# Twenty-four weight loads of an attention and feed-forward kernel: from SyncE's DMA queue to ScalarE's

## The chip, the core and the metric

The kernel runs on one core of a Trainium2 chip. The core has five engines that run side by side: TensorE (PE, matrix products, with its weight loads as PEld), VectorE (DVE), ScalarE (ACT), GpSimd (POOL) and SyncE (SP). SP computes nothing: it issues the transfers between main memory and the core's own memory, and 16 DMA engines carry them out. The metric is the device time of one execution in microseconds (us). Before the change the median of three runs is 685.02 us (681.62, 685.02 and 685.63).

## The reference, cut to what matters

Attention whose mask lets a query see only the keys that fall in the same hash bucket, then two gated feed-forward blocks:

```
q_bits, k_bits = (q @ proj > 0), (k @ proj > 0)          # 6 bits -> bucket
scores = where(q_bucket == k_bucket, q @ k.T / 8, -1e9)  # 2 x 8 heads, 768 x 768
attn   = softmax(scores);  x = attn @ v                  # head_dim 64
x = reshape(x, (1536, 512))
h = x @ w_in;  x = (h * sigmoid(h)) @ w_out              # 512 -> 2048 -> 512
a, b = x @ w1, x @ w2;  x = ((a * b) @ w3) @ w_out2      # 512 -> 1024 -> 1024 -> 512
```

## The kernel before, in words

The program is written as a list of some 2,900 small operations (`op(...)`), each with the engines that it may run on, what it depends on and which buffers it takes and gives back. No scheduler orders them at build time: a table of numbers, `ORDER`, gives the order in which they are written out, and a string, `ON`, gives each one's engine (P, A, D, G, S for PE, ACT, DVE, POOL, SP; N for none). `Plan.run` walks both. Every engine then works through its own operations strictly in that order; semaphores hold an operation back until what it needs is there.

The attention goes over eight pairs of heads, 12 tiles of 128 queries a pair. For each tile PE makes the scores (L763) into one of two `score` buffers, DVE takes the row maximum `st` (L779), ACT takes the exponential `P` (L785, with a short ACTIVATION_READ_ACCUMULATOR that ends it) and so frees the score buffer, and DVE turns `P` over into `pt` (L826). At the end of a pair PE multiplies `pt` with the values `V` (L884), and ACT moves the sums into `X` (L349, L902). Between these stand fillers for PE: the product of two weight matrices, `w3` and `w_out2` (L969), the first parts of the feed-forward (L1252, L1296), and plain transposes (L543).

The weights come in through `piece(...)`. Each half piece is a load of 512 KB (128 rows of 4 KB) into one of two buffers, `raw` (L385). ACT or POOL then reads it (`low`, L403 or L407), ACT reads it again (`high`, L398), and with that the buffer is free for the next load. DVE joins both into `x` (L413), and POOL (now and then ACT) rounds `x` into the two halves of `piece` (L353, L356), from which PE works. So a load into `raw` always waits for the L398 (and, where POOL made `low`, the L407) of the load that held the buffer before.

Before the change SP issues every transfer of the program, in one row: the loads of weights (L385), the queries, keys and values (`qraw`, `kraw`, `V`), the mask rows (`kb<-bits`, `qb<-bits`, L548), copies within the core (L713), the small stores and reads of the inverse sums (`inverse`, `invb`), the product of the weights (`wprime`), and the output. ACT issues none. A transfer that waits on SP holds up the ones behind it.

Of the kernel before, what the change touches and what calls it, by code (L numbers as in the profile page):

```python
# [194 lines left out]
    "ADADDASSSSPPPPPPDDDDAAANAGGGGANAADDPPNPPPPPPPDDDDDNSSSSGGAAAAGGGGGDSGNSSSNPPPPPDDDAAASSAANPPPPPPPNPP"  # L195
    "PPPDDDADDAAAANPPPPDDDDAAAGGGGSSSSSSSPPPPGGGGGDDDDAANAAANPPPNDDGDDDPPPAAANDDDASSNSSSGGGGAADDPPDAPPDDD"
    "GGGAGGAAPDAPDDDPPPAANAASSSNSSPDPPPNPPPDGGGGAAASSSDDDAANPPPPPDDDAAPDAPPPPPGGDDDADDSSSSSSSSSGGGNGGAANA"
    "DPPPDDDAANDDPNAADPDDAASSSSSNSGGAASGGGGPPPPPPDDAPAADDDDGGNPPPPDAANAPPPPPNDDDAASNSSSSSADDDASGGAGGGGGGG"
    "GGPPPPPPPPPPDADDDPDAAAAPPPPDDDDANADDDASSSSSSSSNAANPPPDPNDPPDDNSSSSSSNAAGGGGGGAADPPPPPPPDDDDAGAADAPDP"
    "DDAAAPPPPNPPPPPPPGDDDGGSSDNAAAAAANASSSSGGSSSSGGGGSSSSGPPDDDDAADDPPPPPADDDGGGANAANASPPPGDADANAPPPPNDD"  # L200
    "DDDDPPAANADAPPASSGGGGDDDGPPPPPPSNAAGSSDDDADDPAAADAGGNSSNGGSSSSSSSPPPDDPNDPPPPPPPAANAADDAADDGGGGAANSS"
    "SDPADDPPADAAPPPPPPDDDDSGGGSGGAAAAAANPPPPPNPPPDDDDDDAANDGDSSSSSNSSNAAGDDDPDPDAAAGGGGPDDPDGAAGGAPPPPPP"
    "DDDGAPNPPPDSSSAASSNSSSDDDDPAADPPAAPPPDDDAAGDANADDDADGGGGGPPPPPPPPDDDSSSSSSSGGAANADDSNNSPPNNAGGNGANAD"
    "DDDDAAAPPPPPPADDGGDDPPADPPPPADADDDAAAPPPPPPPSSSSSNSSADDADDAPPPDAGNGGGSSSPPNPAPPPDDDADDPPNPADDAAAPPPP"
# [60 lines left out]
class Plan:  # L265
# [10 lines left out]
    def op(self, on, emit, deps=(), due=0.0, take=(), give=(), size=0, port=False, kind=None, tiled=False):  # L276


        self.ops.append(Op(on, emit, deps, take, give))
        return self.ops[-1]  # L280
# [20 lines left out]
def lsh_attention_moe_kernel(ctx, tc, qT, kT, pair0, v, vt, w3, wo2, win, wo1, w12, out):  # L301
    nc = tc.nc
    ctx.enter_context(tc.manual_schedule())
    engine = {"PE": nc.tensor, "ACT": nc.scalar, "DVE": nc.vector, "POOL": nc.gpsimd, "SP": nc.sync}
    plan = Plan()
    op = plan.op
# [58 lines left out]
    def piece(src, need, wide=True, after=(), duo=False, late=None):  # L365
# [4 lines left out]
        for n in range(0, PIECE, STEP):  # L370
            due = need - 12.0 + 5.0 * n / STEP
            key = name + (n,)
            raw, x, t = key + ("raw",), key + ("x",), key + ("t",)
            first = [("piece", name)] if n == 0 else []
            c = slice(n, n + STEP)
            if wide:
                words = src.bitcast(U32)[:, 2 * n:2 * n + 2 * STEP]
# [7 lines left out]
                load = op({"SP": 400}, lambda e, raw=raw, words=words: nc.sync.dma_start(out=plan[raw], in_=words),  # L385
# [36 lines left out]
            else:  # L422
                load = op({"SP": 400}, lambda e, raw=raw, n=n: nc.sync.dma_start(
                    out=plan[raw].bitcast(F32)[:, :STEP], in_=src(n)), after, due - 10, [("raw", raw)], size=262144, kind="reload")
# [127 lines left out]
    for n in range(B * NPAIR):  # L552
# [4 lines left out]
        raw, hi, lo, ins = {}, {}, {}, []  # L557
# [395 lines left out]
    behind = [w for w, k in WINDOWS for _ in range(k)]  # L953
    after = lambda w: BEGIN + (12 * w + 19) * UNIT
    wo2p = [piece(wo2[i], after(behind[0]) - 8 + i) for i in range(4)]
    combined, before_it = [], None
    span = 5.5
# [248 lines left out]
    for cell in cells:  # L1206
# [75 lines left out]
        for order, (bk, d) in enumerate(turns_):  # L1282
# [29 lines left out]
                else:  # L1312
# [5 lines left out]
                    if halved:  # L1318
                        ev = None
                        for x in range(2):  # L1320
# [6 lines left out]
                            n = bk * 4 + d  # L1327
# [8 lines left out]
                if part == 2 and c == NOUT - 1 and not halved:  # L1336
                    n = bk * 4 + d
# [82 lines left out]
```

## Time and profile before

| | |
|---|---|
| median of three runs | 685.02 us (681.62 to 685.63) |
| the profiled execution, whole | 687.5 us |
| its span, first to last instruction | 685.7 us |
| mean granted TensorE clock | 0.995 |
| busy: PE, DVE, ACT, POOL | 669.0, 516.2, 376.7, 254.0 us |
| DMA moved | 65.3 MB, 95 GB/s on average |

The profile is of one execution. "Busy" leaves out the time in which a sequencer issues a transfer or waits. In a row of a timeline the numbers are start and duration, and what stands in square brackets at the end is the idle time of that engine just ahead, and what ended it. "Issue" there is idle time that ended with no semaphore that the profile shows. The profiled execution lies 2.5 us above the median of the unprofiled runs.

### The profile page before, as it was taken

How to read it: one execution, taken by the hardware profiler on the slowest of the kernel's cores; microseconds unless marked ns; L12 is line 12 of the kernel's file. 1: busy time of each engine (PE TensorE's matmuls, PEld its weight loads, DVE VectorE, ACT ScalarE, POOL GpSimd, SP SyncE). 2: the span in 40 equal slices, each digit the busy share in tenths (PEclk: the TensorE clock that was granted, in tenths of full speed). 3: DMA queues.
4: the chain of work that ended last, by engine and by line, in shares of the span. 5: the costliest groups of instructions: out<-in, count | busy, mean ns of one | idle time of the engine just before them, and what ended most of it. 6: DMA issues, size and time to landing. Idle time of an engine off the chain costs nothing.

```text
span 685.7 us, 13737 instructions
## 1 busy us (share of the span) xinstructions
PE 669.0 (98%) x5542; PEld 544.1 (79%) x5542; DVE 516.2 (75%) x739; ACT 376.7 (55%) x705; POOL 254.0 (37%) x263
## 2 busy tenths in 40 slices
PE   8899998999999999999999999999999999999997
PEld 6558787887787887888888888888887788888886
DVE  6889987796899887967686976778868575545475
ACT  5888776677767564577543553544545454322220
POOL 3668875777578331652200220211222244000000
PEclk9999999999999999999999999999999999999999
DMA  7576645445454611314320221110310012000004
GB/s 228 149 232 179 192 137 155 134 131 184 130 175 108 178 52 54 118 37 147 114 108 1 65 90 47 62 47 1 123 47 31 16 62 77 1 0 16 0 16 168
DMA packets 22031, 65.34 MB, mean 95 GB/s; under 512 B 3408, under 2 KB 4944, under 8 KB 21520
## 3 DMA queue, kind: packets, MB, share of 16 engines
q1 hardware_dynamic: 21968, 64.48, 30.8%
q8 instruction: 43, 0.70, 0.4%
q14 instruction: 20, 0.16, 0.1%
HBM read 55.19 MB, written 5.29 MB: 88 GB/s over the span
## 4 chain that ended last, share of the span: by engine, by line
PE 90%; DVE 5%; ACT 3%; issue 2%; POOL 0%; ACTq 0%; POOLq 0%; DVEq 0%
PE more L1296 21%; PE more L1132 15%; PE more L1252 9%; PE score L763 8%; PE acc L884 7%; PE acc L1296 7%; PE acc L969 6%; PE acc L1132 6%; PE acc L1252 4%; PE turn L884 2%; ACT P L785 1%; DVE st L779 1%; PE acc L850 1%; DVE pt L826 1%; PE acc L543 1%
## 5 line engine op out<-in xcount | busy, mean ns | idle before, releaser
L1132 PE MATMUL more<-y,piece 128*128 128x512 f32 x456 | 115.9, 390 | 0.6 <-DVE y L356 0.3
L785 ACT ACTIVATE P<-score,st 128x768 f32<-128x768 f32 x92 | 82.6, 899 | 41.4 <-DVE st L779 39.5
L779 DVE TENSOR_REDUCE st<-score 128x1 f32<-128x770 f32 x92 | 85.4, 943 | 20.8 <-PE score L763 19.3
L1132 PEld LDWEIGHTS more<-y,piece 128*128 128x128 f32 x456 | 85.4, 188 | 19.3 <-DVE sg L1149 0.9
L1296 PE MATMUL more<-gh,piece 128*128 128x512 f32 x268 | 94.1, 390 | 0.0
L1315 DVE SCALAR_TENSOR_TENSOR X<-more,X 128x512 f32<-128x512 f32 x88 | 59.9, 688 | 40.2 <-PE more L1296 39.6
L826 DVE STREAM_TRANSPOSE pt<-P 128x768 f32<-128x768 f32 x84 | 80.4, 965 | 6.6 <-ACT P L785 6.5
L884 PE MATMUL acc<-pt,V 32*64 32x193 f32 x1344 | 63.6, 328 | 4.9 <-issue 4.5
L884 PE MATMUL turn<-pt,V 32*64 32x193 f32 x1344 | 63.0, 329 | 0.2
L1252 PE MATMUL more<-x,piece 128*128 128x512 f32 x240 | 61.9, 390 | 0.0
L884 PEld LDWEIGHTS acc<-pt,V 32*64 32x64 f32 x1344 | 51.8, 132 | 12.2 <-issue 10.7
L1296 PEld LDWEIGHTS more<-gh,piece 128*128 128x128 f32 x268 | 50.3, 188 | 11.0 <-DVE sg L1198 0.3
L353 POOL TENSOR_SCALAR piece<-x 128x512 fp32r<-128x512 f32 x37 | 23.5, 639 | 83.3 <-DVE x L413 37.1
L1252 PEld LDWEIGHTS more<-x,piece 128*128 128x128 f32 x240 | 45.0, 188 | 9.6 <-DVE X L1315 0.3
L1296 PE MATMUL more<-gl,piece 128*128 128x512 f32 x134 | 52.1, 389 | 0.0
L969 PE MATMUL acc<-piece,piece 128*128 128x512 f32 x192 | 50.6, 401 | 0.0
L763 PE MATMUL score<-ka,qa 128*128 128x384 f32 x168 | 48.2, 369 | 2.4 <-ACT P L785 1.8
L413 DVE SCALAR_TENSOR_TENSOR x<-x,x 128x512 uint32<-128x512 uint32 x59 | 44.3, 754 | 6.2 <-ACT x L398 5.2
L349 ACT ACTIVATE sg<-more 128x512 f32<-128x512 f32 x28 | 16.6, 595 | 57.0 <-PE more L1132 38.0
L884 PEld LDWEIGHTS turn<-pt,V 32*64 32x64 f32 x1344 | 46.7, 132 | 1.4 <-issue 1.3
L1296 PE MATMUL more<-piece,gh 128*128 128x512 f32 x152 | 46.8, 389 | 0.0
L1132 PE MATMUL acc<-y,piece 128*128 128x512 f32 x174 | 45.8, 390 | 0.0
(234 smaller groups left out, 1426.2 us busy)
## 6 DMA issues: line engine op xcount, KB each, us to landing
raw<-in_w SPq DMA_DIRECT2D x27, 512.0 KB
raw<-in_wo SPq DMA_DIRECT2D x22, 512.0 KB
raw<-in_win SPq DMA_DIRECT2D x13, 512.0 KB
V<-in_v SPq DMA_DIRECT2D x14, 384.0 KB
invb<-inverse SPq DMA_DIRECT2D x16, 192.0 KB
out<-X SPq DMA_DIRECT2D x11, 256.0 KB
kraw<-in_kT SPq DMA_DIRECT2D x7, 384.0 KB
qraw<-in_qT SPq DMA_DIRECT2D x7, 384.0 KB
```

The source lines that it names most:

```text
L353: engine[e].tensor_scalar(out=dst, in0=src, scalar1=by, scalar2=1.0, op0=ALU.mult, op1=ALU.mult)
L413: engine[e].scalar_tensor_tensor(out=u32(x), in0=u32(x), scalar=3, in1=u32(t), op0=ALU.logical_shift_left, op1=ALU.bitwise_or)
L763: nc.tensor.matmul(out=sc[:, g, :HF], lhsT=lhs[:k, qs], rhs=rhs[:k, g * HF:g * HF + HF], start=(k == 128), stop=(k != 128),)
L779: nc.vector.tensor_reduce(out=plan[uk("st")][:, 0:1], in_=area()[:, :, :HF + 1], op=ALU.max, axis=AX.XY, negate=True)
L785: nc.scalar.activation(out=plan[uk("P")], in_=area()[:, :, :HF], func=AF.Exp, bias=s[:, 0:1], accum_out=plan[key("sums")][:, par * NQ + i: ...
L826: nc.vector.transpose(plan[mine][:, :, 32 * i:32 * i + 32], plan[uk("P")].rearrange("p g (b i) -> p (g b) i", i=32))
L884: nc.tensor.matmul(out=to[a][64 * side:64 * side + 64, :GW + 1], lhsT=V[rows_, c, side], rhs=plan[key(f"pt{side}")][rows_, c, :GW + 1], st ...
L969: nc.tensor.matmul(out=plan[key + ("ps",)], lhsT=w[:, a, k], rhs=r[:, c], start=(k == 0 and n == 0), stop=(k == 7 and n == 2),)
L1132: nc.tensor.matmul(out=plan[bk[b]], lhsT=w[:, a], rhs=y, start=(opens and j == 0 and m == 0), stop=(j == 1 and m == 2), skip_group_check=True)
L1252: nc.tensor.matmul(out=plan[key], lhsT=w[:, a], rhs=x, start=(k == 0 and n == 0), stop=(k == 3 and n == 2))
L1296: nc.tensor.matmul(out=plan[key], lhsT=a, rhs=x, start=(f == 0 and n == 0), stop=(f == 1 and n == 2))
L1315: nc.vector.scalar_tensor_tensor(out=dst, in0=plan[key], scalar=by, in1=dst, op0=ALU.mult, op1=ALU.add)
```

## The change

Twenty-four of the loads at L385 get the letter A in place of S, so ScalarE's sequencer issues them, on ScalarE's DMA queue. The load operation may now run on either engine:

```diff
-                load = op({"SP": 400}, lambda e, raw=raw, words=words: nc.sync.dma_start(out=plan[raw], in_=words),
+                load = op({"SP": 400, "ACT": 400}, lambda e, raw=raw, words=words: engine[e].dma_start(out=plan[raw], in_=words),
```

(the same for the reload at L423, of which none moves). In `ORDER` the 24 numbers stand earlier; one line of it:

```diff
-    917, 178, 116, 889, 896, 908, 909, 910, 115, 187, 918, 911, 897, 180, 184, 898, 899, 20, 900, 189, 16, 901, 231,
+    917, 178, 116, 889, 896, 908, 909, 910, 931, 115, 938, 187, 918, 911, 897, 180, 184, 898, 899, 20, 900, 189, 16,
```

The moved loads are those that SP issued between 51 and 237 us of the profiled execution: 12 of `w3`, 6 of `w_in`, 6 of `w_out`. The rows of PE, DVE and POOL are the same before and after, and so are all other rows of ACT and SP in their order.

On ACT, in the fourth pair of heads: a load of `w3` stands between the last reader of `raw` (L398) and the next exponential (L785). `P`, `st`, `sums`, `score` are the tiles of the attention, `wsb` holds a finished block of the weight product.

```order
 L785 ACTIVATE P_118,sums_124<-score_82,st_122 128x768
 L398 ACTIVATE x_94<-raw_92 128x512
+L385 DMA raw_92<-in_w 128x1024
 L785 ACTIVATE P_117,sums_124<-score_83,st_120 128x768
 L349 ACTIVATE wsb_97<-acc_405 128x512
```

The load came from SP, where it stood behind other transfers; its place is now right behind the instruction that frees its buffer, ahead of an exponential.

On ACT, about 161 to 166 us, two loads among four exponentials:

```order
 L403 ACTIVATE x_94<-raw_91 128x512
 L398 ACTIVATE x_96<-raw_91 128x512
+L385 DMA raw_91<-in_wo 128x1024
 L785 ACTIVATE P_118,sums_124<-score_83,st_121 128x768
 L785 ACTIVATE P_117,sums_124<-score_82,st_120 128x768
 L398 ACTIVATE x_95<-raw_92 128x512
+L385 DMA raw_92<-in_win 128x1024
 L785 ACTIVATE P_118,sums_124<-score_83,st_122 128x768
 L403 ACTIVATE x_94<-raw_91 128x512
```

Again each load follows the L398 that read its buffer, with an L785 right behind it.

On SP, about 86 to 96 us, the place that two of these loads leave (`kb` and `qb` are mask rows, `ka` a copy of keys, `inverse` the small store):

```order
 L548 DMA qb_111<-bits_108 12x384 x2
 L548 DMA inverse<-wsb_97 12x128
-L385 DMA raw_91<-in_w 128x1024
-L385 DMA raw_92<-in_w 128x1024
 L548 DMA kb_115<-bits_108 12x384
 L713 DMA ka_113<-ka_113 64x768
```

The mask row and the copy of keys no longer stand behind two loads that wait for ACT.

## Rows read from the trace of the kernel before

**Rows 1.** The page: busy time of each engine, and the chain that ended last.
```profile
PE 669.0 (98%) x5542; PEld 544.1 (79%) x5542; DVE 516.2 (75%) x739; ACT 376.7 (55%) x705; POOL 254.0 (37%) x263
...
PE 90%; DVE 5%; ACT 3%; issue 2%; POOL 0%; ACTq 0%; POOLq 0%; DVEq 0%
```

**Rows 2.** Busy time (instructions) in one stretch: PE, PEld, DVE, ACT, POOL, then clock, DMA.
```profile
50.00:237.00 187.00, 180.90 (x2946) 150.10 (x2939) 160.70 (x200) 136.41 (x268) 134.13 (x122) 0.98 0.53 152
```

**Rows 3.** Waits, 50 to 240 us: engine, releaser, us in total, times, longest; PE, ACT, POOL.
```profile
PE acc L884 <- issue: 3.9, 2, 2.2
PE score L763 <- ACT P L785: 1.8, 5, 0.6
...
ACT P L785 <- DVE st L779: 34.4, 37, 4.1
...
POOL x L407 <- DMA raw<-in_w: 0.2, 1, 0.2
```

**Rows 4.** The moved loads on SP by tile: durations of the issue in ns, minimum/median/maximum.
```profile
L385 SPq DMA_DIRECT2D raw<-in_w x12: 328/340/1034, 51.4 to 133.2; - x12
...
L385 SPq DMA_DIRECT2D raw<-in_wo x6: 327/350/537, 156.4 to 236.1; - x6
```

**Rows 5.** Timeline of SP's queue: start, duration (waits inside a merged row included).
```profile
66.24 0.33 SPq L385 DMA_DIRECT2D raw<-in_w  x1
66.64 0.76 SPq L548 DMA_DIRECT2D kb<-bits  x1
...
88.11 5.79 SPq L385 DMA_DIRECT2D raw<-in_w  x2
```

**Rows 6.** Timeline of ACT at places where a load comes to stand.
```profile
65.55 0.66 ACT L398 ACTIVATE x<-raw 128x512 f32<-128x512 f32 x1
66.46 0.90 ACT L785 ACTIVATE P<-score,st 128x768 f32<-128x768 f32 x1 [0.25 <-DVE st L779]
67.26 0.19 ACT L785 ACTIVATION_READ_ACCUMULATOR P<-score,st 128x1 f32 x1
...
92.87 0.66 ACT L398 ACTIVATE x<-raw 128x512 f32<-128x512 f32 x1
93.43 0.89 ACT L785 ACTIVATE P<-score,st 128x768 f32<-128x768 f32 x1
94.21 0.20 ACT L785 ACTIVATION_READ_ACCUMULATOR P<-score,st 128x1 f32 x1
...
159.62 0.20 ACT L785 ACTIVATION_READ_ACCUMULATOR P<-score,st 128x1 f32 x1
...
163.13 0.19 ACT L785 ACTIVATION_READ_ACCUMULATOR P<-score,st 128x1 f32 x1
...
208.59 0.19 ACT L785 ACTIVATION_READ_ACCUMULATOR P<-score,st 128x1 f32 x1
```

**Rows 7.** Timeline of ACT: places with idle time behind the load's new place.
```profile
54.24 0.84 ACT L349 ACTIVATE ka<-ka 64x768 fp32r<-64x768 f32 x1 [1.24 <-POOL ka L353]
...
135.59 0.90 ACT L785 ACTIVATE P<-score,st 128x768 f32<-128x768 f32 x1 [2.69 <-DVE st L779]
```

**Rows 8.** Timeline of PE: the scores that follow those exponentials.
```profile
67.51 0.61 PE L763 MATMUL score<-ka,qa 128*128 128x384 f32 x2 [0.17 <-ACT P L785]
...
94.46 0.62 PE L763 MATMUL score<-ka,qa 128*128 128x384 f32 x2 [0.32 <-ACT P L785]
...
159.96 0.53 PE L763 MATMUL score<-ka,qa 128*128 128x384 f32 x2
...
163.57 0.62 PE L763 MATMUL score<-ka,qa 128*128 128x384 f32 x2
...
208.84 0.62 PE L763 MATMUL score<-ka,qa 128*128 128x384 f32 x2 [0.58 <-ACT P L785]
```

**Rows 9.** Busy time in two stretches, columns as in rows 2: a gap of PE, and after it.
```profile
105.20:107.45 2.25, 0.01 (x1) 0.00 (x0) 1.03 (x3) 0.24 (x2) 0.00 (x0) 1.00 1.01 368
108.60:112.20 3.60, 3.60 (x17) 3.40 (x12) 2.06 (x3) 2.56 (x8) 2.56 (x4) 0.53 0.46 124
```

More of the change, by code (lines that the diff above doesn't have):

```diff
@@ L194 @@
     "SSSSSSGGGDAPANDDANDAAGAANPPPGADDDSSSSSSSSSSSAAANGGNSSPNDADDGAPPAANPPADDDDPPPPDDGGSAANDDGGGAADDAAANPP"
[L195 to L204, printed above, removed]
+    "ADADDASSSSPPPPPPDDDDAAANAGGGGANAAAADDPPNPPPPPPPDDDDDNSSGGAAAAGGGGGDSGNSSSNPPPPPDDDAAASSAANPPPPPPPNPP"
+    "PPPDDDAADDAAAANPPPPDDDDAAAAGGGGSSSSSPPPPGGGGGDDDDAANAAANPPPNDDGDDDPPPAAAANDDDAASSNSGGGGAADDPPDAPPDDD"
+    "GGGAGGAAPDAPDDDPPPAANAAASSSNSSPDPPPNPPPDGGGGAAASSSDDDAANPPPPPDDDAAAPDAPPPPPGGDDDADDSSSSSSSGGGNGGAANA"
+    "ADPPPDDDAANDDPNAAADPDDAASSSNSGGAASGGGGPPPPPPDDAPAADDDDGGNPPPPDAANAPPPPPNDDDAASNSSSSSADDDASGGAGGGGGGG"
+    "GGPPPPPPPPPPDAADDDPDAAAAPPPPDDDDANAADDDASSSSSSSNAANPPPDPNDPPDDNSSSSSNAAGGGGGGAADPPPPPPPDDDDAGAAADAPD"
+    "PDDAAAPPPPNPPPPPPPGDDDGGSDNAAAAAANAASSSSGGSSSGGGGSSSSGPPDDDDAADDPPPPPADDDGGGANAANAAPPPGDADANAAPPPPND"
+    "DDDDDPPAANADAPPASSGGGGDDDGPPPPPPNAAGSSDDDADDPAAADAAGGNSSNGGSSSSSSPPPDDPNDPPPPPPPAANAADDAADDGGGGAAANS"
+    "SDPADDPPADAAAPPPPPPDDDDSGGGGGAAAAAANPPPPPNPPPDDDDDDAAANDGDSSSSSNSSNAAGDDDPDPDAAAAGGGGPDDPDGAAGGAPPPP"
+    "PPDDDGAPNPPPDSAASSNSSSDDDDPAADPPAAPPPDDDAAGDANAADDDADGGGGGPPPPPPPPDDDSSSSSSGGAANADDSNNSPPNNAGGNGAANA"
+    "DDDDDAAAPPPPPPAADDGGDDPPADPPPPADADDDAAAPPPPPPPSSSSNSADDADDAPPPDAGNGGGSSSPPNPAPPPDDDADDPPNPADDAAAPPPP"
     "PPANADDNDAANASSSDGGDDDADDSNNADAADPPPDDPPPPPADAAAADPPPPDDDDDAAADDDDPPGDPPPPADPPPNDPADDDAADDPPPPPPGSSA"
@@ L422, in piece @@
             else:
-                load = op({"SP": 400}, lambda e, raw=raw, n=n: nc.sync.dma_start(
+                load = op({"SP": 400, "ACT": 400}, lambda e, raw=raw, n=n: engine[e].dma_start(
                     out=plan[raw].bitcast(F32)[:, :STEP], in_=src(n)), after, due - 10, [("raw", raw)], size=262144, kind="reload")
```

74 rows, old and new, of the table ORDER are left out of this document.

## The prediction

> **What bounds the kernel now.** I read the page first: PE is busy for 669.0 of 685.7 us, and 90% of the chain that ended last is PE's own work [rows 1]. PE's order is fixed by hand and does not change, so the end can move only by time in which PE stands idle, or runs at the lower clock. The table of stretches then says how much of that there is where the 24 loads move, 50 to 237 us: PE works 180.9 of 187.0 us, so 6.1 us are idle; ACT works 136.4 us and has 50.6 us of room [rows 2]. The list of waits says what ended PE's idle time there: 3.9 us in two gaps inside the products with V that no semaphore ended, and 1.8 us in five waits of a score for ACT's exponential [rows 3]. The rest are pauses too short for the list. ACT in turn waits mostly for the row maximum, 34.4 us before 37 of its exponentials, and in this stretch for no transfer at all; POOL waits for a weight load once, 0.2 us [rows 3]. So the loads as they are issued today are late for nobody that matters.
>
> **The change part by part.** *What SP loses.* 24 issues of a median 0.34 or 0.35 us [rows 4], and the time in which they blocked its queue: at 88.11 us two loads hold SP for 5.79 us, since the second waits for ACT's reader [rows 5]. The mask rows, keys and values behind them start up to some 5 us sooner. No engine but POOL waits for such a transfer in this stretch, and PE never, so I price this at 0. If PE did wait for them unseen, it could be no more than the pauses that the list of waits does not explain, 6.1 - 3.9 - 1.8 = 0.4 us.
>
> *Earlier loads.* Each is now issued right when its buffer comes free, so it lands no later than today. What follows it (the split on ACT and POOL, the weight product on PE) waits for it for 0.2 us in all [rows 3]. Also 0, with -0.2 us as the other end, and that on POOL.
>
> *What ACT gains as work.* No transfer is issued from ACT in this trace, so the price is bounded. The nearest rows are the same loads on SP. SP issues the load at 66.24, 0.03 us after the reader L398 has ended (65.55 + 0.66 = 66.21), takes 0.33 us, and starts its next transfer 0.07 us after that, at 66.64 [rows 5, 6]. On ACT the load must likewise wait for the reader's end, and the next activation stands behind it: 0.03 + 0.34 + 0.07 = 0.44 us from the end of L398 to the next start. Where ACT runs back to back it also loses an overlap: the exponential at 93.43 begins 0.10 us before the L398 at 92.87 has ended (93.53) [rows 6], so there the loss is 0.54 us. The lower end is 0: ACT's room takes it all. The upper end is the longest of these issues, 1.03 us [rows 4], which adds 0.69 us a place. I take 0.44, since the same form moves the same bytes.
>
> The Trainium skill bears on this price (Perfetto Trace Analysis, Per-instruction lifecycle): a transfer issued from SP or ACT first locks the descriptor generator, which the issuing sequencers share, and the profile's duration includes that lock wait. By the page an ACT load that meets an issue of SP would be longer by what is left of it; nothing in the trace of before can show it, as one engine alone issues. By it the sum below would be larger, which is the third rival.
>
> *Which of these delays reach PE.* I went through the 24 places on ACT's timeline. At seven, ACT idles at least as long behind the load anyway, at most 2.69 us; that one is shown [rows 7]. They cost nothing. At twelve more the next score that needs the exponential starts well after it has ended, or another wait of ACT (such as 1.24 us for POOL behind the first two loads [rows 7]) takes up the delay. At five places the score on PE follows the exponential's end (start + duration of the READ_ACCUMULATOR) closely:
> - load after 66.21: the exponential has 0.25 us of idle time; it would start at 66.65, not 66.46: 0.19 us late. It ends at 67.45, PE starts at 67.51 and waited for it [rows 6, 8]. Passes 0.19.
> - load after 93.53: 0.54 late; ends at 94.41, PE at 94.46. Passes 0.54.
> - load after 156.4, ahead of the copy of V and two exponentials, all back to back: 0.54; ends at 159.82, PE at 159.96, of which some 0.05 is the semaphore (as at 94.41 to 94.46). Passes 0.45.
> - load after 162.4: 0.54; ends at 163.32, PE at 163.57. Passes 0.34.
> - load after 206.9: 0.54; ends at 208.78, PE at 208.84. Passes 0.54.
>
> Sum 2.06, say +2.1 us. PE cannot win it back: behind 237 us nothing in its order is cut, and it goes on working without a pause most of the time. The profiled span would go from 685.7 to 687.8 and that execution from 687.5 to 689.6; against the median of the runs shown, which lies 2.5 us lower, 685.0 + 2.1 = 687.1 us.
>
> **The rivals.**
> 1. *All hidden.* ACT's 50.6 us of room and the 34.4 us of waiting speak for it; five waits of PE on the exponential speak against. It gives 685.0 us.
> 2. *Faster: the gaps of PE go.* At 105.20 PE stops for 2.25 us among the products with V while the DMA engines are fully busy (share 1.01, 368 GB/s), and after it the granted clock is 0.53, between 108.60 and 112.20 [rows 9], so mostly at the lower level, 1.2 GHz. That costs 0.47 x 3.60 = 1.7 us more. Two gaps make 3.9 us and, if the second is like the first, 3.4 us of slow clock: 7.3 us. If the gaps come from the crowd of transfers on one queue, loads issued elsewhere and earlier may thin it out. One gap gone gives 687.1 - 3.65 = 683.5, both 679.8 us. Against it: the bytes stay, and ACT would issue the two loads around 102 to 105 us no earlier than SP does. The reverse, one more gap, gives 690.8 us.
> The Trainium skill (Runtime: NRT & Kernel Launch, Instruction fetch mechanics) says that the engine streams its instructions by DMA in blocks while it executes, the cost mostly hidden; by that page there would be no such gap to lose or win, yet the trace has two.
> 3. *Slower: ACT's issues are long.* SP issues small transfers in the same microseconds, and one such issue takes 0.76 us [rows 5]. If a load on ACT had to sit out one each time, each place would lose 0.76 us more; the five above and about four with little slack (behind 75, 77, 88 and 188 us) would pass it: 9 x 0.76 + 2.1 = 8.9, or 693.9 us. It decides from an issue of about 1.2 us on ACT. Against it: back to back issues on SP do not stretch that far at the median.
> 4. *The change does nothing it says*, since the loads were on time: then only ACT's price is left, which is the forecast.
>
> **How the numbers follow.** The forecast (five places pass part of 0.54 us): 0.58. All hidden: 0.15. One or both gaps gone: 0.10. Long issues: 0.12. One more gap: 0.05. The three runs of before already spread over 4.0 us, about one gap. The range takes in one gap gone with some spread (683.0) up to one gap more (691.5), and leaves out both gaps gone and most of the long issues; the forecast's own range is 685 to 690, from nothing passed to 1.03 us an issue. About 1%, 6.9 us, is what a measurement of this kernel can tell from no change: below 678.2 only both gaps gone together with hidden issues would come, 0.03; above 691.9 most of the third rival and two more gaps, 0.13; the rest, 0.84, is within 1%.
>
> **What would show it.** In the profile of after: 24 issues on ACT of about 0.34 us, the next activation about 0.1 us behind each; the list of waits with more than 1.8 us of PE on the exponential, or fewer and later scores near 94, 160, 164 and 209 us; PE's place in the program about 2 us later at the end of the attention and the same distance later at the end. Wrong would be: issues on ACT over 0.7 us (rival 3), no shift of PE at these places (rival 1), or a different number of gaps with no releaser, each followed by a stretch at the lower clock (rival 2).

## The result, and the profile after

| | before | after |
|---|---|---|
| median of 15 runs each | 685.19 us (681.62 to 689.57) | 690.84 us (689.24 to 692.72) |
| ratio, 95% interval | | 1.0087 (1.0067 to 1.0107) |
| the profiled execution, whole / span | 687.5 / 685.7 us | 689.52 / 687.7 us |

The change costs 5.65 us, 0.8 to 0.9%. The forecast was 2.1 us. The profiled execution of before lay above its median and that of after lies below its own, so the two traces differ by only 2.0 us; where they are compared below, it is place by place. The mean granted clock, which is on record for every execution, bears on this: the trace of before has 0.995, as low as only 13 of 87 executions of that kernel beside the experiments, the trace of after 1.000. Among executions at 1.000 the means are 683.2 us before (26 of 87) and 690.2 us after (7 of 15). So at full clock the change costs some 7 us, and the trace of before shows more of the low clock than most executions of its kernel.

The page of after: busy time of the engines, the chain that ended last, and two of the queues (q10 is ACT's, q8 carries blocks of PE's instructions).

```profile
PE 667.7 (97%) x5542; PEld 541.4 (79%) x5542; DVE 516.5 (75%) x739; ACT 376.8 (55%) x705; POOL 253.9 (37%) x263
...
q10 hardware_dynamic: 3456, 12.58, 6.1%
q8 instruction: 43, 0.70, 0.4%
...
PE 69%; DVE 3%; DMA 1%; issue 1%; ACT 1%; ACTq 0%; DVEq 0%
```

The busy times are within 1.3 us of those before [rows 1]; the 24 loads are the 12.58 MB on q10. New in the chain is DMA: the end now also depends on transfers.

The stretch of rows 2, and the waits of rows 3, after (engine, releaser, us in total, times, longest):

```profile
50.00:237.00 187.00, 178.35 (x2933) 146.42 (x2932) 159.44 (x199) 134.58 (x265) 132.15 (x119) 1.00 0.53 150
```
```profile
PE turn L884 <- issue: 3.5, 4, 1.5
...
PE score L763 <- ACT P L785: 2.7, 6, 0.8
...
ACT wsb L349 <- DMA inverse<-wsb: 1.8, 1, 1.8
...
PE acc L884 <- issue: 1.2, 2, 0.6
...
ACT wsb L349 <- DMA wprime<-wsb: 1.1, 1, 1.1
PE acc L884 <- ACT wsb L349: 0.9, 2, 0.7
```

PE is idle for 187.00 - 178.35 = 8.65 us of this stretch, 2.55 us more than before [rows 2]. The list names three parts: gaps in L884 without a releaser 4.7 us in six (3.9 in two before), scores that wait for the exponential 2.7 (1.8 before) [rows 3], and a wait that before did not have, 0.9 us for ACT's `wsb`. Against this the clock is 1.00 throughout; before it was 0.53 of full speed behind a gap [rows 9].

The 24 issues on ACT by tile: durations in ns, minimum/median/maximum.

```profile
L385 ACTq DMA_DIRECT2D raw<-in_w x12: 334/334/389, 49.4 to 133.3; - x12
...
L385 ACTq DMA_DIRECT2D raw<-in_win x6: 334/334/335, 143.1 to 223.1; - x6
L385 ACTq DMA_DIRECT2D raw<-in_wo x6: 334/334/335, 157.3 to 236.5; - x6
```

They are as short as on SP [rows 4]. ACT's timeline at the second and the fifth place that the forecast charged:

```profile
93.75 0.67 ACT L398 ACTIVATE x<-raw 128x512 f32<-128x512 f32 x1
94.44 0.33 ACTq L385 DMA_DIRECT2D raw<-in_w  x1
94.83 0.90 ACT L785 ACTIVATE P<-score,st 128x768 f32<-128x768 f32 x1 [0.41 <-ACT x L398]
...
206.85 0.42 ACT L902 ACTIVATE X<-turn,fv 128x192 f32<-128x192 f32 x1
206.85 0.34 ACTq L385 DMA_DIRECT2D raw<-in_win  x1
207.17 0.41 ACT L902 ACTIVATE X<-turn,fv 128x192 f32<-128x192 f32 x1
```

At 94.44 the load waits for the L398 right ahead of it, which frees its buffer; ACT then stands idle for 0.41 us (0.03 + 0.33 + 0.05). At 206.85 the buffer is already free: the load goes out while an activation runs, and the next activation starts on time. Of the 24 loads 13 are of the first kind, one costs 0.2 us, and ten cost nothing.

PE's timeline at the five scores of rows 8:

```profile
66.99 0.62 PE L763 MATMUL score<-ka,qa 128*128 128x384 f32 x2 [0.33 <-ACT P L785]
...
95.87 0.62 PE L763 MATMUL score<-ka,qa 128*128 128x384 f32 x2 [0.78 <-ACT P L785]
...
161.12 0.61 PE L763 MATMUL score<-ka,qa 128*128 128x384 f32 x2
...
165.18 0.62 PE L763 MATMUL score<-ka,qa 128*128 128x384 f32 x2 [0.29 <-ACT P L785]
...
209.55 0.62 PE L763 MATMUL score<-ka,qa 128*128 128x384 f32 x2 [0.59 <-ACT P L785]
```

The first, second and fourth wait longer than before, the fifth as long as before. PE's distance from its place in the trace of before grows from 0.87 to 1.26 us over the four scores from 160.24 to 161.57, so 0.39 there, and by 0.35 at 165.18.

And the new wait: the chain that ended with PE's product at 194.78 (start, us, what).

```profile
185.38 4.49 DMA wprime<-wsb
...
189.95 0.28 ACT wsb L349
...
190.24 3.78 DMA inverse<-wsb
...
194.13 0.61 ACT wsb L349
...
194.78 0.37 PE acc L884
```

`wsb` is a single buffer. Two stores of it, one after the other, hold up ACT's next block and so PE. SP's queue in the trace of before, where each store stands ahead of a load, and then ACT's queue after, where the loads go out 0.56 and 0.21 us ahead of the stores of the chain above:

```profile
187.30 0.34 SPq L548 DMA_DIRECT2D wprime<-wsb  x1
187.69 0.43 SPq L385 DMA_DIRECT2D raw<-in_wo  x1
...
191.11 0.33 SPq L548 DMA_DIRECT2D inverse<-wsb  x1
191.48 0.35 SPq L385 DMA_DIRECT2D raw<-in_win  x1
```
```profile
184.82 0.34 ACTq L385 DMA_DIRECT2D raw<-in_wo  x1
...
190.03 0.33 ACTq L385 DMA_DIRECT2D raw<-in_win  x1
```

By the packets in the traces: before, the first of these stores had ended 1.66 us after its issue; after, 4.09 us. The second: 1.02 us before, 3.00 us after. Over the five `inverse` stores of the attention, the median from issue to the last packet went from 1.09 to 2.81 us. So the loads had been behind these stores and now are ahead of them; whether the loads' bytes make the stores late is tested below.

### The profile page after: what moved, and what is told of

It is laid out like the page before. It is cut to its first block, busy times and chain, and to the rows that moved or that the text cites. A ratio compares the mean times of both kernels' runs of the same rounds, so it can differ in the third digit from the quotient of the medians.

```text
span 687.7 us, 13715 instructions
## 1 busy us (share of the span) xinstructions
PE 667.7 (97%) x5542; PEld 541.4 (79%) x5542; DVE 516.5 (75%) x739; ACT 376.8 (55%) x705; POOL 253.9 (37%) x263
## 3 DMA queue, kind: packets, MB, share of 16 engines
q10 hardware_dynamic: 3456, 12.58, 6.1%
## 4 chain that ended last, share of the span: by engine, by line
PE 69%; DVE 3%; DMA 1%; issue 1%; ACT 1%; ACTq 0%; DVEq 0%
PE more L1296 21%; PE more L1132 15%; PE more L1252 8%; PE acc L1296 7%; PE acc L1132 6%; PE acc L1252 4%; PE acc L884 4%; PE score L763 2%; PE turn L884 1%; DVE st L779 1%; DVE pt L826 1%; DMA wprime<-wsb 1%; DMA inverse<-wsb 1%; PE acc L969 0%; DVE piece L356 0%
## 5 line engine op out<-in xcount | busy, mean ns | idle before, releaser
L785 ACT ACTIVATE P<-score,st 128x768 f32<-128x768 f32 x92 | 82.7, 900 | 38.4 <-DVE st L779 34.4
L884 PE MATMUL acc<-pt,V 32*64 32x193 f32 x1344 | 63.5, 325 | 3.6 <-issue 2.4
L884 PE MATMUL turn<-pt,V 32*64 32x193 f32 x1344 | 62.2, 325 | 3.5 <-issue 3.5
L884 PEld LDWEIGHTS acc<-pt,V 32*64 32x64 f32 x1344 | 51.5, 130 | 10.8 <-issue 7.7
L884 PEld LDWEIGHTS turn<-pt,V 32*64 32x64 f32 x1344 | 46.9, 130 | 5.2 <-issue 5.2
```

Of the source, the lines that this page charges most:

```text
L785: nc.scalar.activation(out=plan[uk("P")], in_=area()[:, :, :HF], func=AF.Exp, bias=s[:, 0:1], accum_out=plan[key("sums")][:, par * NQ + i: ...
L884: nc.tensor.matmul(out=to[a][64 * side:64 * side + 64, :GW + 1], lhsT=V[rows_, c, side], rhs=plan[key(f"pt{side}")][rows_, c, :GW + 1], st ...
```

## The experiments

Four theories were weighed: 1, ACT's own time for the issues; 2, small transfers that land late behind the loads; 3, the new places, whatever the queue; 4, PE's gaps in L884. All runs had the kernel before beside them on the same chip (685.28 to 686.33 us median). A ratio is to that, with its 95% interval. Not all runs were on one chip, so a difference that is not a ratio may be across chips.

### The two halves of the change, each alone

In `e1_order_only` the 24 numbers stand at their new places, with S in `ON`; in `e2_act_old_place` at their old places, with A.

> The 24 loads stand at the new, earlier places of the order, but SP still issues them all, so ACT issues nothing. Theory 1 (ACT's own time: 0.41 us of ACT per issued load, passed on to PE at a few places): the cost is gone, 685 us, ratio 1.000. Theory 2 (two queues: a load on ACT's queue shares the 16 DMA engines with SP's small transfers, which land later, and their readers wait): one row again, also 1.000. Theory 3 (the earlier place itself crowds the transfers): 690.8 us, ratio 1.008, as the whole change. If SP's row is now held up by loads that wait for their buffer earlier in it, slower still, over 1.008.

> The 24 loads keep their old places in the order, but ACT issues them. Theory 1 (ACT's time): ACT pays the same 24 times 0.41 us, so about the whole cost stays, 688 to 691 us, ratio 1.004 to 1.009. Theory 2 (two queues): the loads still overtake SP's small transfers and share the engines with them, 689 to 691, ratio 1.006 to 1.009. Theory 3 (the place): 685, ratio 1.000.

Measured: `e1_order_only` 715.55 us, ratio 1.044 (1.0405 to 1.0474). `e2_act_old_place` 692.33 us, ratio 1.0089 (1.0058 to 1.0120). PE's waits in the first, ACT's in the second, 50 to 240 us:

```profile
PE score L763 <- DMA qb<-bits: 14.0, 3, 6.7
```
```profile
ACT x L403 <- DMA raw<-in_w: 8.8, 3, 5.9
```

The new places are no good for SP: a load that waits for its buffer holds the mask rows behind it, and PE waits 14.0 us for them. The old places are no good for ACT: nearly every load there goes out under a running activation, for nothing, but ACT comes to some of them late (the load that SP issued at 126.84 us goes out at 138.31), and ACT then waits for its own loads. So the second run's 0.9% is not the change's 0.9%: its list shows another way, in which ACT waits for loads. Neither half explains the whole.

### ACT's time alone

`e3_act_time` leaves the loads on SP and gives ACT the time. `e3b_act_time_512` differs in the size of the scratch tile only.

```diff
             o.emit(ENGINES[e])
+            for _ in range(2 * EXTRA.count(n)):
+                self.idle()
...
+    scr = wp.tile([128, 48], F32, name="scr")                # e3b: wp.tile([128, 128], ...)[:, :48]
+    plan.idle = lambda: nc.scalar.activation(out=scr, in_=scr, func=AF.Copy, scale=1.0)
```

> The kernel before, all loads on SP at their old places; at each of the 24 places where the changed order has a load on ACT, two small activations (128x48 in place on a scratch tile, about 0.21 us each by the rows of 128x1 at 0.17 and 128x512 at 0.62) take about 0.42 us of ACT's time. Theory 1 in the size of the forecast: +2.1 us, 687.1, ratio 1.003; if ACT's time is the whole of the measured cost: +5.7, 690.8, ratio 1.008. Theories 2 and 3 alone (queues, place): ratio 1.000.

> As the run with the small activations in place of ACT's issues, but the scratch tile takes 512 bytes a partition in place of 192, so that the buffers behind it keep the alignment that they have before. In the run with 192 bytes the stretch from 290 us on, where nothing was changed, was 9 us longer at a clock of 1.00 (a matrix product of 512 columns took 395 ns in place of 390). If that came from the place of the buffers, it is gone here, and what is left is ACT's time in the attention alone: theory 1 in the forecast's size 687 to 688, ratio 1.003; if ACT's time is the whole cost of the change 691, ratio 1.008; if ACT's time costs nothing 685 to 686, ratio 1.000.

Measured: 693.20 us, ratio 1.0124 (1.0081 to 1.0167), and with 512 bytes 685.61 us, ratio 1.0028 (1.0000 to 1.0057). The first one's excess is in the feed-forward, where nothing was changed. PE's products of 512 columns there, 300 to 650 us, in the first and in the second:

```profile
L1303 PE MATMUL more<-gh,piece 128*128 128x512 f32 x240 | 85.4, 395 | 0.0
```
```profile
L1303 PE MATMUL more<-gh,piece 128*128 128x512 f32 x240 | 84.1, 390 | 0.0
```

So the first run is spoilt by its tile and says nothing of ACT. The second gives ACT 48 x 0.24 = 11.5 us more work at the 24 places, more than the loads themselves take, and costs 0 to 0.6% (1.9 us at 1.0028). PE's waits for the exponential rise to 3.4 us there, so ACT's time does reach PE; it is not the 5.65 us, though 1.9 us is near the forecast's 2.1.

### The loads' traffic

`e7_thin_on_act` and `e7_thin_on_sp` are the kernels after and before with the 24 loads cut to an eighth of their bytes:

```diff
+                few = slice(0, 128 if len(plan.ops) in THIN else 2 * STEP)
-... .dma_start(out=plan[raw], in_=words)
+... .dma_start(out=plan[raw][:, few], in_=words[:, few])
```

> The changed kernel; each of the 24 loads brings 512 bytes a row in place of 4 KB, so an eighth of its traffic (the rest of raw keeps old values, and the weights made from it are wrong). ACT's issues stay. Theory 4 (PE's gaps in L884: the fetch of PE's next 256 instructions starts late where loads fill the DMA engines; 4.75 us of gaps in the profiled run after) and theory 2 (late stores, about 1 us): both go, 685 or less, ratio 1.000 or below. Theory 1 (ACT's time is all): 690 to 691, ratio 1.008.

> The kernel before with the same 24 loads cut to an eighth, still issued by SP. Theory 4: the gaps of the kernel before (2.25 and 1.63 us in the profiled run, each with a stretch at half clock) go too: 680 to 681.6, ratio 0.993. What then still lies between this run and the same loads on ACT is ACT's issue time with no traffic in it: 2 us by the forecast's sum. If PE's gaps are not a matter of the loads' traffic: 685 to 686, ratio 1.000, with gaps as before.

Measured: on SP 681.13 us, ratio 0.9940 (0.9917 to 0.9963), all 12 runs between 679.08 and 682.45 where those of before beside them went from 679.88 to 690.10. On ACT 683.79 us, ratio 0.9998 (0.9978 to 1.0018). PE's waits on SP, then on ACT, 50 to 240 us:

```profile
PE acc L886 <- issue: 2.2, 2, 1.4
PE score L765 <- ACT P L787: 1.7, 5, 0.5
```
```profile
PE score L765 <- ACT P L787: 3.0, 6, 0.8
PE turn L886 <- issue: 2.7, 3, 1.4
```

This pair splits the cost. With little traffic the step from SP to ACT costs 683.79 - 681.13 = 2.66 us, of which 1.3 us stand in the list as waits for the exponential and 0.5 as gaps. The loads' bytes cost 685.28 - 681.13 = 4.15 us where SP issues them, and 690.84 - 683.79 = 7.05 us where ACT does: 2.90 us more. So by the medians about half of the 5.65 us is ACT's part and half is what the same bytes do at another time. The halves are rough: by resampling the recorded times the first is 1.8 to 3.9 us and the second 1.3 to 4.8, and by the ratios, each good to some 1.5 us, they are 4.0 and 2.0 us.

The wait for `wsb` is gone with the bytes. In the trace of `e7_thin_on_act` the same two stores, issued 0.56 and 0.57 us behind their thin loads, ended after 1.71 and 0.98 us, as in the trace of before. So it is the loads' bytes, and not the issue on ACT, that made them late. The gaps in L884 got shorter with thin loads (2.2 and 2.7 us in place of 3.9 and 4.7) but did not go.

### A buffer for the small store

`e4_own_store` is the changed kernel, `c4_before_own_store` the kernel before, each with:

```diff
+    plan.buffers("isb", tiles(wp, "isb", [128, 128], F32, 1))
-                un = op({"ACT": act(128)}, unload, [fl], te + 4, [("wsb", key("invt"))], [key("it")])
+                un = op({"ACT": act(128)}, unload, [fl], te + 4, [("isb", key("invt"))], [key("it")])
```

> The changed kernel, with a buffer of its own (isb, 128x128) for the small inverse sums that so far share the single wsb with the blocks of the weight product. ACT's block of the product then waits no more for the store of the sums. Theory 2, in the part that the trace after names (PE's L884 waits 0.9 us in all for ACT's wsb, whose store lands late): 0.9 us less than the change, 689.9, ratio 1.007; if late stores are most of the cost, 687 or less, ratio 1.003. Theory 1 (ACT's time): 690.8, ratio 1.008, no gain.

> The kernel before with the separate 512-byte buffer for the inverse sums, the control of the same edit to the changed kernel (687.3). If ACT's wait for the late store of the sums is a cost of the change alone (theory 2), nothing happens here: 685 to 686, ratio 1.000. If the buffer helps by something else, the kernel before gains as much: 682 to 683, ratio 0.996.

Measured: the changed kernel 687.32 us, ratio 1.0029 (1.0004 to 1.0054); the kernel before 686.00 us, 1.0005 (0.9972 to 1.0038). The buffer helps after (1.0029 against 1.0087 for the change) and not before, so the late store is a cost of the change. PE's waits with the buffer in the changed kernel, all that are listed:

```profile
PE turn L885 <- issue: 4.6, 4, 1.5
PE score L764 <- ACT P L786: 2.7, 6, 0.8
```

The waits for the exponential are as after; those for `wsb` are gone. The gaps in L884 add up to 4.6 us still, so with all of them the kernel is at 0.29%: the gaps are not the bulk of what the change costs. By the medians the gain is 3.5 us, more than the 0.9 us of listed waits. Place by place in the two traces PE wins 1.6 us between 191 and 199 us, and 0.8 us from a gap at 203.7 that is no longer there; how the rest comes about was not settled, and this part overlaps with the 2.90 us above.

### PE's gaps in L884

`e9_shifted` is the changed kernel with 16 more transposes at the very start.

```diff
-        for _ in range(14):
+        for _ in range(30):
             nc.tensor.transpose(turn[:, 0, :128], ident, ident)
```

> The changed kernel with 16 more transposes among those at the start that wake PE, while PE waits for the first data, so that every later matrix product stands 16 further in PE's row of instructions. Theory 4 (PE stops at the end of each 256 instructions that were fetched): the gaps in L884 keep their place by count (the 729th, 1110th, 1238th, 1746th product in PE's row, one after a multiple of 128 of the same stretch), so they fall 16 products earlier in the program than after the change. If something in the program at that place makes PE wait, they move with the program, to the 745th, 1126th, 1254th and 1762nd. The time is that of the change, 690 to 692, if the gaps' sizes stay.

Measured: 689.65 us, ratio 1.0065 (1.0039 to 1.0091). The first two gaps, after and here:

```profile
79.06 0.38 PE L884 MATMUL turn<-pt,V 32*64 32x193 f32 x2 [1.45 <-issue]
...
103.47 0.39 PE L884 MATMUL turn<-pt,V 32*64 32x193 f32 x4 [0.81 <-issue]
```
```profile
79.87 0.38 PE L884 MATMUL turn<-pt,V 32*64 32x193 f32 x2 [1.43 <-issue]
...
104.37 0.39 PE L884 MATMUL turn<-pt,V 32*64 32x193 f32 x4 [0.89 <-issue]
```

Counting PE's products from the start of the trace (0 is the first), the gaps stand ahead of numbers 729, 1110, 1238 and 1746 in both, although in the second everything behind the start is 16 products further on. So the gaps go by the count of instructions and not by the program. 1238 - 1110 = 128 products and as many weight loads are 256 instructions. The packets of q8 give the rest; each is 16 KB (43 packets, 0.70 MB):

| gap ahead of product | PE passed the boundary 128 before | packet of q8, start to end | PE goes on |
|---|---|---|---|
| before, 1238 (2.25 us) | 100.98 | 104.93 to 106.01 | 107.45 |
| before, 2128 (1.63) | 163.30 | 167.29 to 168.32 | 169.71 |
| before, 729 (none) | 74.23 | 75.82 to 76.80 | 78.14 |
| after, 729 (1.45) | 73.72 | 76.67 to 77.62 | 79.06 |
| after, 1238 (0.60) | 103.47 | 105.90 to 106.83 | 108.30 |
| after, 2128 (none) | 164.56 | 166.40 to 167.35 | 169.40 |

In all runs here, wherever PE stood still in L884 for over 0.3 us between 50 and 240 us, and not for `wsb`, it went on 1.2 to 1.6 us after such a packet had ended (39 gaps in 13 traces). The packet itself takes 0.9 to 2.0 us. What varies most is its start. In the trace of before one began 0.49 us after the boundary at 69.61 us, and one 3.94 us after that at 100.98. The stretches of that trace after the two boundaries, columns as in rows 2 (the last two are the DMA engines' share and GB/s):

```profile
69.70:71.20 1.50, 1.50 (x39) 1.05 (x31) 1.29 (x3) 1.26 (x3) 1.42 (x2) 1.00 0.08 22
...
103.00:106.00 3.00, 2.21 (x85) 1.82 (x84) 2.87 (x5) 2.44 (x6) 0.00 (x0) 1.00 0.91 232
```

Of these two packets the first starts at once and the second late, and there the engines are full of other transfers. How late a packet starts does not follow the share alone: the packet that began at 166.40 in the trace of after came 1.84 us after its boundary, at a share of 1.05. An unbroken run of 128 products of L884 takes 2.8 us (160.76 to 163.57 us before), so a late block stops PE.

The Trainium skill (Runtime: NRT & Kernel Launch, Instruction fetch mechanics) says that each engine streams its instructions in blocks of 16 KiB, 256 instructions, by a DMA queue of its own, the cost mostly hidden. The block agrees with the packets of q8 and with the count; "mostly hidden" does not hold in L884 under full DMA engines.

### Which of the loads

`e5_five` moves only the five loads that the forecast charged, `e6_nineteen` only the others; the rest stay with SP at their old places.

> Only the five loads that the forecast charged (behind the L398 that ended at 66.21, 93.53, 156.4, 162.4 and 206.9 us of the profile before) go to ACT, at their new places; the other nineteen stay on SP at their old ones. The forecast's step (these five places carry all of ACT's time that reaches PE): 687.3 us, ratio 1.003. If the cost comes from the nineteen that were priced at nothing (their ACT time, or the traffic that they bring ahead): 685.3, ratio 1.000. If it comes from these five and the traffic that they bring ahead: 689 to 691, ratio 1.006 to 1.008.

> The other nineteen loads go to ACT, at their new places, and the five that the forecast charged stay on SP at their old ones. The forecast's step (these nineteen are covered): 685.3 us, ratio 1.000. Theory 4 (loads that now stand earlier delay the fetch of PE's instructions at the ends of the pairs) and theory 2 (late stores): their cost of about 3 us comes from these, 688 to 689, ratio 1.004 to 1.006.

Measured: the five 683.96 us, ratio 0.9990 (0.9961 to 1.0020); the nineteen 690.85 us, ratio 1.0093 (1.0063 to 1.0123). The nineteen that were priced at nothing cost as much as all 24, the five nothing that can be measured (at most 0.2%). The five are not quite the forecast's five, though. With the other loads on SP, the two buffers come free in another order, and only two of the five still stand right behind the L398 that they wait for. One that doesn't, on ACT:

```profile
91.24 0.69 ACT L403 ACTIVATE x<-raw 128x512 uint32<-128x512 uint32 x1
91.65 0.34 ACTq L385 DMA_DIRECT2D raw<-in_w  x1
91.82 0.91 ACT L785 ACTIVATE P<-score,st 128x768 f32<-128x768 f32 x1
```

PE's waits with the nineteen, 50 to 240 us:

```profile
PE turn L884 <- issue: 2.7, 3, 1.2
PE score L763 <- ACT P L785: 2.6, 6, 0.6
PE acc L884 <- issue: 2.1, 2, 1.6
PE acc L884 <- ACT wsb L349: 0.9, 2, 0.6
```

They have it all, the late store and 4.8 us of gaps among it; nine of them stand behind their own L398. The scores wait 2.6 us for the exponential here too, although none of the five loads is on ACT: a delay of ACT reaches PE at other places when it does not come at those five.

### Fewer gaps in the kernel before

`e8_late_loads` is the kernel before with three loads one place later in SP's row, behind loads of `V`:

```order
-L385 DMA raw_92<-in_win 128x1024
-L548 DMA V_105<-in_v 32x3072
+L548 DMA V_105<-in_v 32x3072
+L385 DMA raw_92<-in_win 128x1024
```

> The kernel before; three loads that SP issues while PE is in an L884 stretch (101.99, 104.58 and 165.33 us of the profile before, read by ACT or POOL only from 116 us and 181 us on) stand one place later in SP's row, behind the load of V at 108.47 and at 175.56, so out of those stretches. Theory 4 (transfers issued ahead of a fetch delay it, and PE stops where its instructions end): the two gaps of the kernel before shrink to 1.4 and 0.8 us or less, as with the loads cut to an eighth, and the half clock behind them goes: 681 to 683, ratio 0.995. If loads have nothing to do with the gaps: 685.3, ratio 1.000. If the later loads hold up their readers: slower than that.

Measured: 685.67 us, ratio 1.0015 (0.9985 to 1.0044): no gain. The first gap shrank from 2.25 to 1.18 us; the second grew from 1.63 to 2.16 us, and two new ones came (1.1 us together). So the expectation that both would shrink failed:

```profile
167.76 0.38 PE L884 MATMUL acc<-pt,V 32*64 32x193 f32 x2 [2.16 <-issue]
```

Here the packet of q8 began at 165.38 us; the packets of the keys' load `kraw`, issued at 160.84, just as PE passed the boundary (160.83), ended at 165.39. The load that was moved had been issued at 165.33 in the trace of before, 2 us after that boundary, so it was not what the fetch stood behind. No version here that brings all the bytes beat the kernel before.

## Why the prediction was right or wrong

- *The time*: 690.84 us lies in the range, and 3.7 us above the forecast of 687.1. "Within 1%" held. The range reached so far because of "one more gap", a rival with a chance of 0.05 at 690.8 us. That this is the measured time is luck: that rival meant a long gap with a slow clock behind it, and what came was late stores and six short gaps at a clock of 1.00. PE's place in the traces was 1.0 us later at the end of the attention and 1.7 us at the end; the forecast had about 2 both times.
- *The price of an issue* (0.44 us) was right where its ground was: 0.41 us behind the L398 that frees the buffer. That every load pays it was wrong: ten of 24 go out under a running activation.
- *The five places*: the first four passed 0.16, 0.46, 0.39 and 0.35 us (forecast 0.19, 0.54, 0.45, 0.34), the fifth nothing (0.54), since its load found a free buffer. So 1.36 of the 2.06 us came where the forecast had put them. The size of this term was nearly right (ACT's part is 1.9 us in `e3b_act_time_512`, 2.7 in the thin pair), but not that these five places alone carry it: without them the scores waited as long in `e6_nineteen`.
- *Earlier loads, "also 0"*: this is the step that failed. It asked who waits for the loads, and not what the loads now stand ahead of. The stores of `wsb` used to be ahead of them in SP's row; their packets ended after 4.1 and 3.0 us in place of 1.7 and 1.0, and that passed through a single buffer to ACT and PE (`e4_own_store`). The blocks of PE's instructions met the loads at other boundaries: six gaps, 4.7 us, at a clock of 1.00 in place of two, 3.9 us, with slow stretches behind. That these cost more than the old ones is not shown. `e5_five` and `e6_nineteen` agree: the loads that were priced at nothing cost the 0.9%, and the charged ones none that can be measured. What the bytes add by the thin pair, 2.90 us, holds the late stores and whatever the gaps add to them.
- *Rival 2* named the crowd of transfers as a cause of the gaps and took their number for the open question. That the loads' bytes lengthen the gaps is borne out: with thin loads on SP, 4.15 us faster in all, they went from 3.9 to 2.2 us in the traces. In the trace of after one old gap went, the other shrank to 0.60 us, their slow clock went, and six short gaps came in all; the time was not won.
- *Rival 3* fell: issues on ACT took 0.334 us at the median and 0.389 at most, though 13 of the 24 overlapped an issue on SP. The Trainium skill (Perfetto Trace Analysis, Per-instruction lifecycle) would have them longer where SP issues at the same time; no run here shows that on this scale.
- *Rival 1* (all hidden) and *rival 4* (only ACT's price is left) fell with the measured cost.

What stays open: how the 2.90 us divide between late stores and gaps, which move one another; and how many gaps an unprofiled execution has, since each kernel has one trace. The recorded clocks tell of slow stretches alone: by an estimate from rows 9 one such stretch takes 0.0025 off the mean clock (0.47 x 3.60 of 685.7 us), and 0.998 or less stands on 51 of 87 executions before and 7 of 15 after. So the change does not plainly rid the kernel of them, as the two traces alone would suggest.

## What to carry to other kernels

Before a transfer is moved to another queue, list what it was queued behind: on its own queue those transfers went first here, and the small store that now comes second is what the path may hang on. An issue on ScalarE was free where it did not depend on the activation that was running, and cost 0.41 us of idle time right behind the instruction that frees its buffer, so the earliest place for a load was also the dear one. Where PE idles with no releaser among many short products, count 256 instructions and look at the instruction queue's packets.

## What was not expected of the hardware

- PE's instructions come in packets of 16 KB; in L884 (256 instructions in 2.8 us without a gap) PE stood still for up to 2.5 us where a packet came late; at the 14 gaps of over 1.3 us it had started 2.8 to 4.7 us after the boundary before.
- A store on one queue came late behind bytes that had been issued just earlier on another: 6 KB issued 0.21 us after a load of 512 KB on the other queue ended 3.00 us later, 1.02 us without a load ahead of it, and 0.98 us behind a load cut to an eighth.
- A scratch tile of 192 bytes a partition ahead of the other buffers made the products of 512 columns take 395 ns in place of 390, at a clock of 1.00, and the feed-forward about 9 us longer; with 512 bytes it was 390 ns again. Why the place matters was not looked into.
